# Attention's P times V after every unit of the gated feed-forward, in place of every second unit

## The chip, the cores and the metric

The kernel runs on one core of one Trainium2 chip. Its metric is the device time of one execution in microseconds (us); the kernel before has a median of 2574.44 us over three runs (2574.06 to 2574.53). A core has a matrix engine (TensorE, PE in the profile, with its weight loads shown apart as PEld), a vector engine (VectorE, DVE), an activation engine (ScalarE, ACT), GpSimd (POOL), and SyncE (SP), whose queue issues most of the DMAs here.

## The reference

The input x has 2048 rows of 576 features. It is normalized (layer norm without weights), and the normalized rows feed two branches: softmax attention with 32 heads of 18 features, and a gated feed-forward with 4608 hidden features.

```
xn = layernorm(x)
q, k, v = split(xn @ wqkv)                    # 32 heads of 18
p = softmax(q k^T * 18**-0.5)                 # 2048 x 2048 for each head
s = (p v) @ wo
h = relu(xn @ W_gate) * (xn @ W_up)           # 4608 wide
g = silu(h @ W_down)
out = x + s * g
```

Everything is float32. Most products are taken as three products of split operands (a high part and a rest), which is why each product of the feed-forward shows up three times.

## The kernel before

The program has three stages. The first normalizes the rows, turns them and computes q, k and v, which go to DRAM. The last projects the attention's output with wo, multiplies by the gate and adds x. The long middle stage, from about 200 to 2500 us, runs attention and feed-forward interleaved. All of the change lies there.

**Units.** The feed-forward is cut into 144 units: four groups of 512 rows by 36 blocks of 128 hidden features (`units`). Function `emit_unit` (lines 937 to 992) emits one unit k. It opens with weight loads and splits, then interleaves on TensorE the unit's gate and up products (`up`, tile `pg`, two chains of 27 matmuls that run on the two 64-row halves of the array) with attention work: matmuls of scores for the row maxima of the next head pair (`max_steps`, tile `pm`, reduced by VectorE into `mx`) and matmuls of scores for the exponentials of the present head pair (`exp_steps`, tile `psx`, then an exponential on ScalarE into a tile `p`). A list of due times worked out in `emit_unit` fixes the order. The prediction calls this an up stretch. Then `up_end` applies relu on ScalarE and multiplies on VectorE (line 740), which gives the tile `h`, later split into `hh` (line 747 and GpSimd).

**Rounds of two units.** After the up stretch, what follows depends on whether k is odd or even. For an even k, `down(k - 1)` (line 754) multiplies the hidden features of the two units k - 2 and k - 1 by W_down: 96 matmuls in eight chains (tile `py`), with marks on ScalarE (line 781) where a chain changes banks, and additions of the results into `y` (VectorE at line 797; one of four blocks by ScalarE and GpSimd). For an odd k, `attend` (line 920) empties the list `ready`.

**P times V.** In units 16 to 143 each head pair u takes eight units. Each unit completes four key tiles of 128 keys: for each, the exponentials of two heads by two blocks of 512 queries, in one tile `p` of four parts. `exp_steps` appends such a tile to `ready`. `attend` takes one and issues four matmul calls, one for each part, whose outputs lie in four strips of 32 partitions of one PSUM bank (`po`):

```
for s_ in range(4):
    h = s_ // 2
    mm(
        po[0][s_ * 32 : s_ * 32 + 32, :], va[:, kt, h * VA : h * VA + 32], pt[:, s_, :],
        start=(kt == 0), stop=(kt == NT - 1), skip_group_check=True,
    )
```

As the operands are float32, each call is two matmuls in the profile, so a key tile is eight, in two groups of four that run side by side. Sixteen key tiles make half a head pair (1024 queries); after the last, `finish` copies `po` on ScalarE and puts the rest (transposes, a reciprocal and a product on VectorE, lines 877 to 887) into the list `outs`, which runs just ahead of the next P times V. The stores of the finished block go through the list `later`, which the next `emit_unit` runs (`run_later`).

**What fixes the order.** TensorE's matmuls, VectorE's operations in this stage, GpSimd's operations and a part of ScalarE's are held to program order. The exponentials are not, until the last head pair (`ac`), and SP's DMAs are not after unit 17; a scheduler places these at compile time. The tiles `p` come from a pool of eight buffers (line 688), `po` has one PSUM bank (line 108), and the score and down tiles share five (line 107).

Of the kernel before, what the change touches and what calls it, by code (L numbers as in the profile page):

```python
# [19 lines left out]
def kernel(  # L20
# [46 lines left out]
    def mm(*args, **kw):  # L67
        return tc.keep_in_program_order(nc.tensor.matmul(*args, **kw))  # L68
# [217 lines left out]
    def load_up(k):  # L286
        if k < len(units):
            f = units[k][1]
            if 2 < k < N1:
                rgs[k] = as_rg(pp.tile([P, 4, 512], F32, name="p"))  # L290
            else:
                rgs[k] = wr.tile([P, KC, P], F32, name="rg")
            load2(rgs[k], [[(wg, f * P, P)], [(wu, f * P, P)]])

    def split_up(k):
        if k in rgs:
            gus[k] = ws.tile([P, 2, KC, P], F32R, name="gw")
            split_pool(gus[k][:, 0], gus[k][:, 1], rgs.pop(k))
# [393 lines left out]
    def load_down(k):  # L692
        if k < len(units):
            f = units[k][1]
            if k == 1:
                rds[k] = hp.tile([P, 2, 512], F32, tag="hh", name="rd", bufs=3)
                rds[k] = rds[k].rearrange("p a s -> p (a s)")[:, :D]
            else:
                rds[k] = wl.tile([P, D], F32, name="rd", bufs=1)
            sp.dma_start(rds[k], wd[f * P : (f + 1) * P, :])  # L700

    def split_down(k):
        dws[k] = wl.tile([P, 2, D], F32R, name="dw")
        split_pool(dws[k][:, 0], dws[k][:, 1], rds.pop(k))

    def up(k):

        g, f = units[k]
        gw = gus.pop(k)
        if k < N1 and (k % 2 == 0 or k == N1 - 1):  # L710
            ps = [psO.tile([P, 512], F32, name="po"), shared("pg2")]
        else:
            ps = [bank("pg0"), bank("pg1")]
        last = f == NF - 1 and k + 1 < len(units)
        if f == NF - 2 and k + 2 < len(units):
            for c in range(2):
                load_x(units[k + 2][0], c)
        xg = xcur[g]

        def ops(t, c, i, j, rows):  # L720
            return gw[rows, i, c, :], xg[c][rows, j, :]

        def half(t):
            for n, _ in enumerate(row_half(ps[t], ops, t)):
                c = n // len(PRODUCTS)
                if t and last and n % len(PRODUCTS) == 2 and c + 2 < KC:
                    load_x(units[k + 1][0], c + 2)
                    if c == KC - 3:
                        load_up(k + 2)
                yield  # L730

        return ps, [half(t) for t in range(2)]

    def up_end(k, ps):
        g, f = units[k]
        if f == NF - 1 and k + 1 < len(units):
            del xcur[g]
        h = hp.tile([P, 512], F32, name="h", bufs=1)
        ac.activation(h, ps[0], AF.Relu)
        vec(nc.vector.tensor_tensor(h, ps[1], h, ALU.mult))  # L740
        between.append((split_h, (k, h)))
# [62 lines left out]
    def gate_step(spill_=True):  # L804
        if gates:
            y, t = gates.pop(0)
            e = wl.tile([P, D], F32, name="e", bufs=1)
            tc.keep_in_program_order(nc.scalar.activation(e, y, AF.Tanh, scale=0.5))
            gp.tensor_scalar(e, e, 0.5, 0.5, op0=ALU.mult, op1=ALU.add)
            gp.tensor_tensor(y, y, e, ALU.mult)  # L810
            if spill_:
                gp.dma_start(gd[t * P : (t + 1) * P, :], y)
# [14 lines left out]
    def run_later():  # L827
        while later:
            later.pop(0)()

    outs = []

    def run_tasks(todo):
        while todo:
            fn, args = todo.pop(0)
            fn(*args)
# [34 lines left out]
    def finish(po, u, p):  # L871
        ot = block32("ot")
        ac.activation(ot, po, AF.Copy)

        def rest_():
            tq = block32("tq")
            vec(nc.vector.transpose(tq, ot))
            tv = tq.rearrange("p (c d) -> p c d", d=32)
            rc = two.tile([P, 16], F32, name="rc")
            vec(nc.vector.reciprocal(rc, tv[:, :, DH]))  # L880
            vec(
                nc.vector.tensor_tensor(
                    tv[:, :, :DH], tv[:, :, :DH], rc.unsqueeze(2).to_broadcast([P, 16, DH]), ALU.mult
                )
            )
            on = block32("on")
            vec(nc.vector.transpose(on, tq))
            later.append(lambda: store(on, u, p))

        outs.append((rest_, ()))  # L890

    ready = []
# [27 lines left out]
    def attend():  # L920

        va, u, p, kt, pt = ready.pop(0)
        if kt == 0:
            po[0] = psO.tile([P, 512], F32, name="po")
# [6 lines that stand above are left out]
        if kt == NT - 1:  # L931
            finish(po[0], u, p)
# [4 lines left out]
    def emit_unit(k, ex, ns, mx, nm):  # L937
        if k - 1 in rds:
            split_down(k - 1)
        if k == len(units) - 2:  # L940
            split_up(k + 1)
            out_weights(4)
        if k not in rds and k not in dws:
            load_down(k)
        if k == 0:
            load_down(1)
        split_up(k + 1)
        if k and (units[k][1] < NF - 1 or k + 1 == len(units)):
            load_up(k + 2)
        if k == N1 + 1:  # L950
            sp.kept = False
        run_later()
        if k % 2:
            if k in rds:
                split_down(k)
            for _ in range(2):
                if to_load:
                    out_weights(to_load.pop(0))
        n = KC * len(PRODUCTS) + ns + nm
        ps, gens = up(k)  # L960
        order = []
        for t in range(2):
            due = []
            for cnt, gen, off, late in ((nm, mx, 0.0, LATE), (ns, ex, 0.25, -4)):
                due += [((i + off + t * 0.5) * (n - 1 + late) / cnt, gen[t]) for i in range(cnt)]
            due.sort(key=lambda d: d[0])
            ops = [gens[t]] * n
            free = n
            for when, gen in reversed(due):
                free = min(round(when), free - 1)  # L970
                ops[free] = gen
            order.append(ops)
        for i, (l, r) in enumerate(zip(*order)):
            next(l)
            next(r)
            if i == 8 or (i == 30 and k % 2 == 0):
                gate_step()
        if k == 0:
            split_up(2)
        up_end(k, ps)  # L980
        if k % 2 or k == 0:
            run_tasks(between)
        if k == 0:
            pinned(nc.scalar.activation(first_exp, ident[:, :1], AF.Exp))
        run_tasks(tasks)
        if k % 2:
            run_tasks(outs)
            while ready:
                attend()
        elif k:  # L990
            down(k - 1)


# [2 lines left out]
    def out_weights(c):  # L996
        rd = wl.tile([P, D], F32, name="rd", bufs=1)
        if c < 4:
            sp.dma_start(rd, wo[c * P : (c + 1) * P, :])
            w = kq.rearrange("p c s -> p (c s)")[:, c * 2 * D : (c + 1) * 2 * D]  # L1000
        else:
            for d in range(2):
                sp.dma_start(rd[d * DT : (d + 1) * DT, :], wo[C4:D, :])
            w = wr.tile([P, 2 * D], F32R, tag="rg", name="wo4")
        w = w.rearrange("p (i d) -> p i d", i=2)
        split_pool(w[:, 0], w[:, 1], rd)
        wos.append(w)
# [68 lines left out]
    k = 0  # L1076
    for n in FIRST:
        if 4 <= k < 4 + NQ:
            load_k(1, k - 4)
        emit_unit(k, None, 0, mx, n)  # L1080
        k += 1
    for u in range(NU):
# [8 lines left out]
        for i in range(PER):  # L1091
            if not more and i == 0:
                to_load[:] = range(4)
            emit_unit(k, ex, 64 // PER, mx, 64 // PER if more else 0)
            if not more:
                if i == 3:
# [77 lines left out]
```

## Time and profile before

| What | Value |
| --- | --- |
| Median of three runs | 2574.44 us |
| The profiled execution's own time | 2574.45 us |
| Its span, first to last instruction | 2572.7 us |
| TensorE busy, instructions | 2565.1 us, 25301 |
| P times V on TensorE (`po` from `p` and `va`) | 4096 matmuls, 452.7 us busy |
| Gate and up products (`pg`), the largest group | 1359.2 us busy |
| Down products (`py`) | 478.1 us busy |
| VectorE, ScalarE, GpSimd busy | 1852.5, 1473.8, 1286.7 us |

A row of a group gives the line, the engine, the operation, the tiles written and read with their sizes, the count, the busy time in us with the mean of one in ns, and then the idle time ahead of them. Busy time counts time in which at least one instruction of the group runs, so matmuls that run side by side are counted once, and the mean of one can be longer than its share. A row of the timeline gives the start, the length from the first start to the last end, the engine and the operation, with neighbours of one kind put together (x64). Matmul ends are modelled; the starts are what the arguments here use.

### The profile page before, as it was taken

The numbers are of one execution on the slowest core, as the hardware profiler recorded it, in microseconds if no ns is written. First come the engines' busy times: TensorE is split into PE (matmuls) and PEld (weight loads), VectorE is DVE, ScalarE is ACT, GpSimd is POOL, SyncE is SP. The second block draws the span as 40 slices with busy tenths as digits, with TensorE's granted clock in tenths as the row PEclk, the third lists the DMA queues.
The fourth block names the chain that finished last, engine by engine and source line by source line (L and its number), as shares of the span: only waits on it lengthen the run. The fifth ranks groups of instructions, "written<-read, shape, count | busy, mean of one in ns | idle before, by whom it ended". The sixth has DMA issues, their size and how long they took to land.

```text
span 2572.7 us, 61560 instructions
## 1 busy us (share of the span) xinstructions
PE 2565.1 (100%) x25301; PEld 2039.7 (79%) x25301; DVE 1852.5 (72%) x3019; ACT 1473.8 (57%) x3005; POOL 1286.7 (50%) x1035
## 2 busy tenths in 40 slices
PE   9999999999999999999999999999999999999999
PEld 8889997777777777777777777777777777777788
DVE  5336677777877788877777777887777877778136
ACT  3222146666666666666666666666666666666652
POOL 4246764444465444444465454444445445454554
PEclk9999999999999999999999999999999999999999
DMA  7864432333542223232353232322354332322246
GB/s 249 293 206 126 110 88 51 79 74 76 125 115 68 72 69 75 58 78 65 97 140 85 69 77 63 77 71 63 75 131 107 74 76 66 79 52 59 70 135 199
DMA packets 263833, 253.55 MB, mean 99 GB/s; under 512 B 27648, under 2 KB 208896, under 8 KB 263552
## 3 DMA queue, kind: packets, MB, share of 16 engines
q1 hardware_dynamic: 255808, 222.48, 34.2%
q0 software_dynamic: 7744, 27.14, 3.1%
q8 instruction: 199, 3.26, 0.5%
q14 instruction: 82, 0.67, 0.1%
HBM read 203.01 MB, written 46.01 MB: 97 GB/s over the span
## 4 chain that ended last, share of the span: by engine, by line
PE 98%; DVE 1%; POOL 0%; DMA 0%; issue 0%; ACT 0%; SPq 0%; POOLq 0%; ACTq 0%
PE pg L68 33%; PE po L68 18%; PE py L68 18%; PE pm L68 10%; PE psx L68 10%; PE pq L68 3%; PE pw L68 2%; PE pv L68 2%; PE tps L76 0%; DMA qd<-hh 0%; DMA xt<-in_A_x_dram 0%; POOL gw L85 0%; DVE hh L129 0%; DVE wqk L645 0%; DVE xn L374 0%
## 5 line engine op out<-in xcount | busy, mean ns | idle before, releaser
L273 DVE TENSOR_REDUCE mx<-pm 128x1 f32<-128x512 f32 x2048 | 1372.2, 690 | 355.2 <-PE pm L68 180.8
L68 PE MATMUL pg<-x,gw 64*128 64x512 f32 x7533 | 1359.2, 392 | 0.0
L97 ACT ACTIVATE p<-psx 128x512 f32<-128x512 f32 x2048 | 1097.2, 604 | 202.4 <-PE psx L68 161.7
L68 PEld LDWEIGHTS pg<-x,gw 64*128 64x128 f32 x7533 | 1028.9, 186 | 80.5 <-issue 1.9
L85 POOL TENSOR_TENSOR hh<-h,hh 128x512 fp32r<-128x512 f32 x144 | 185.8, 1290 | 802.5 <-ACT hh L747 798.7
L68 PE MATMUL py<-dw,hh 64*128 64x288 f32 x6912 | 478.1, 293 | 0.0
L68 PEld LDWEIGHTS py<-dw,hh 64*128 64x128 f32 x6912 | 472.8, 184 | 5.4 <-ACT h L97 0.6
L68 PE MATMUL po<-p,va 128*32 128x512 f32 x4096 | 452.7, 594 | 0.0
L68 PEld LDWEIGHTS po<-p,va 128*32 128x32 f32 x4096 | 126.5, 110 | 291.2 <-issue 280.0
L85 POOL TENSOR_TENSOR gw<-rg,gw 128x1152 fp32r<-128x1152 f32 x131 | 349.8, 2670 | 10.5
L797 DVE TENSOR_TENSOR y<-py,y 128x288 f32<-128x288 f32 x422 | 171.8, 453 | 139.3 <-PE py L68 139.2
L68 PE MATMUL psx<-qT,kq 56*128 56x512 f32 x608 | 231.1, 392 | 0.0
L68 PE MATMUL pm<-kq,qT 54*128 54x512 f32 x608 | 225.4, 395 | 0.0
L85 POOL TENSOR_TENSOR dw<-rd,dw 128x576 fp32r<-128x576 f32 x144 | 206.2, 1432 | 11.5
L68 PE MATMUL psx<-kq,kA 56*128 56x512 f32 x512 | 195.8, 393 | 0.0
L68 PE MATMUL psx<-kq 56*128 56x512 f32 x512 | 194.7, 392 | 0.0
L68 PE MATMUL pm<-kA,kq 54*128 54x512 f32 x512 | 191.5, 396 | 0.3 <-DVE mx L273 0.3
L68 PE MATMUL pm<-kq 54*128 54x512 f32 x512 | 191.1, 396 | 0.0
L781 ACT ACTIVATE mark<-ident 128x1 f32<-128x1 f32 x288 | 58.4, 203 | 218.3 <-PE py L68 218.2
L85 POOL TENSOR_TENSOR y<-add,y 128x576 f32<-128x576 f32 x61 | 87.3, 1432 | 187.4 <-ACT add L97 182.0
L85 POOL CAST gw<-rg 128x1152 fp32r<-128x1152 f32 x131 | 154.5, 1179 | 51.0 <-DMA rg<-in_B_W_up_dram 20.6
L747 ACT ACTIVATE hh<-h 128x512 fp32r<-128x512 f32 x144 | 90.7, 630 | 123.9 <-DVE h L740 123.9
(106 smaller groups left out, 2559.3 us busy)
## 6 DMA issues: line engine op xcount, KB each, us to landing
rd<-in_B_W_down_dram SPq DMA_DIRECT2D x144, 288.0 KB
rg<-in_B_W_gate_dram SPq DMA_DIRECT2D x131, 288.0 KB
rg<-in_B_W_up_dram SPq DMA_DIRECT2D x131, 288.0 KB
x<-xTd SPq DMA_DIRECT2D x72, 256.0 KB
qd<-hh POOLq DMA_DIRECT2D x16, 512.0 KB, 4.5
kd<-hh POOLq DMA_DIRECT2D x16, 512.0 KB, 5.8
xTd<-x SPq DMA_DIRECT2D x16, 512.0 KB
kq<-kd SPq DMA_DIRECT2D x210, 36.0 KB
```

Of the source, the lines that this page charges most:

```text
L68: return tc.keep_in_program_order(nc.tensor.matmul(*args, **kw))
L85: return lambda *args, **kw: tc.keep_in_program_order(op(*args, **kw))
L97: i = op(*args, **kw)
L273: vec(nc.vector.tensor_reduce(mx[:, h, b, j, c : c + 1], ps, axis=AX.X, op=ALU.max))
L747: copy = nc.scalar.activation(hhs[k][:, 0], h, AF.Copy)
L781: seen.append(pinned(nc.scalar.activation(mark, ident[:, :1], AF.Copy)))
L797: vec(nc.vector.tensor_tensor(ys[j][:, cs], outs_[m], ys[j][:, cs], ALU.add))
```

## The change

In `emit_unit`, the list `outs` and all of `ready` are worked off at the end of every unit. The down product of an even unit stays, and now follows the unit's P times V. A unit leaves four key tiles in `ready`, so each P times V has four key tiles (32 matmuls in the profile) where every second unit had eight (64).

```
         run_tasks(tasks)
-        if k % 2:
-            run_tasks(outs)
-            while ready:
-                attend()
-        elif k:
+        run_tasks(outs)
+        while ready:
+            attend()
+        if k % 2 == 0 and k:
             down(k - 1)
```

The units before 16 have nothing in `ready` or `outs`; for them nothing is different.

## The prediction

> **What bounds the kernel now.** I read the first page of the profile, then the waits of TensorE, then one round of two units cut into stretches, and last the timeline at the places where TensorE changes from one kind of work to another.
>
> ```profile
> span 2572.7 us, 61560 instructions
> ...
> PE 2565.1 (100%) x25301; PEld 2039.7 (79%) x25301; DVE 1852.5 (72%) x3019; ACT 1473.8 (57%) x3005; POOL 1286.7 (50%) x1035
> ...
> PEclk9999999999999999999999999999999999999999
> ...
> PE 98%; DVE 1%; POOL 0%; DMA 0%; issue 0%; ACT 0%; SPq 0%; POOLq 0%; ACTq 0%
> ...
> L97 ACT ACTIVATE p<-psx 128x512 f32<-128x512 f32 x2048 | 1097.2, 604 | 202.4 <-PE psx L68 161.7
> ...
> L68 PE MATMUL po<-p,va 128*32 128x512 f32 x4096 | 452.7, 594 | 0.0
> ```
>
> TensorE is on 98% of the chain that ended last and its clock is never throttled. A modelled busy share of 100% doesn't say that no time is lost between matmuls, so the view of TensorE's own waits comes next, and one round (all busy times in us; the columns are PE, PEld, DVE, ACT, POOL, clock, DMA share, GB/s).
>
> ```profile
> PE warm L76 <- POOL ident masks.py:199: 1.4, 1, 1.4
> PE tps L76 <- DVE xn L374: 1.3, 2, 1.0
> PE pm L68 <- DVE mx L273: 0.3, 1, 0.3
> ```
>
> ```profile
> 1311.82:1318.24 6.42, 6.42 (x98) 6.42 (x98) 4.48 (x10) 2.04 (x6) 5.48 (x5) 1.00 0.14 39
> 1318.24:1328.65 10.41, 10.41 (x90) 8.39 (x86) 9.23 (x15) 9.86 (x20) 7.42 (x6) 1.00 0.50 125
> 1328.65:1335.65 7.00, 7.00 (x65) 1.98 (x64) 5.10 (x8) 0.91 (x2) 6.51 (x7) 1.00 0.66 168
> 1335.65:1345.80 10.15, 10.15 (x90) 8.33 (x87) 8.71 (x14) 9.19 (x18) 7.01 (x7) 1.00 0.37 96
> ...
> 1379.93:1413.60 33.67, 33.67 (x334) 25.83 (x332) 28.09 (x45) 21.12 (x42) 15.84 (x11) 1.00 0.29 72
> ```
>
> These are the three largest of the five rows of its waits: TensorE waits for other engines under 4 us in the whole run. A round is: the down product (6.42), an up stretch with scores in it (10.41 here, less in most rounds), a burst of P times V over eight key tiles (7.00), another up stretch (10.15). A typical round takes 33.67. So the time is the sum of TensorE's own work, and a change counts by what it does to the spacing of matmuls. The number of matmuls stays the same; what changes is how often TensorE passes between the up or down work, which uses 64-row tiles, and P times V, which uses tiles of 32 columns.
>
> **The change, part by part: what a burst costs beside its matmuls.** These are starts and lengths on TensorE: first the passage from an up stretch to the down product, then into the burst.
>
> ```profile
> 1311.59 0.44 PE L68 MATMUL pm<-kA,kq 54*128 54x512 f32 x2
> 1311.83 6.61 PE L68 MATMUL py<-dw,hh 64*128 64x288 f32 x96
> ...
> 1328.34 0.39 PE L68 MATMUL pm<-kA,kq 54*128 54x512 f32 x1
> ...
> 1329.11 5.33 PE L68 MATMUL po<-p,va 128*32 128x512 f32 x48
> ```
>
> Then the end of the burst and the next up stretch, with the weight loads of the same place below.
>
> ```profile
> 1334.26 1.47 PE L68 MATMUL po<-p,va 128*32 128x512 f32 x12
> 1335.66 0.50 PE L68 MATMUL pm<-kq 54*128 54x512 f32 x1
> ...
> 1336.00 0.39 PE L68 MATMUL psx<-qT,kq 56*128 56x512 f32 x1
> ...
> 1336.46 0.39 PE L68 MATMUL pm<-kq 54*128 54x512 f32 x1
> ```
>
> ```profile
> 1335.66 0.18 PEld L68 LDWEIGHTS pm<-kq 54*128 54x128 f32 x1 [0.84 <-issue]
> ...
> 1335.77 0.19 PEld L68 LDWEIGHTS psx<-qT,kq 56*128 56x128 f32 x1
> ```
>
> The regular step: in the up stretch two row halves run side by side, and from 1336.00 to 1336.46 lie two steps, 0.23 each. From up to down the step is 1311.83 - 1311.59 = 0.24, so this passage costs nothing today. In the burst four matmuls run side by side; 48 take 5.33 and 12 take 1.47, so nine groups of four take 3.86, one 0.429.
>
> Into the burst: it starts at 1328.65 (the third stretch above), 0.31 after the last matmul of the up stretch, 0.08 over the regular step. Out of it: sixteen groups by 0.429 are 6.86, while the stretch to the first up matmul is 7.00: 0.14 goes into filling and emptying. And the first pair after it is longer: 1336.00 - 1335.66 = 0.34 in place of 0.23, 0.11 more. The weight rows show why: no weight load begins for 0.84 until the burst has left the array, and the second load starts only at 1335.77, where elsewhere loads run ahead under the matmuls. One visit to P times V thus costs 0.08 + 0.14 + 0.11 = 0.33 us over its matmuls.
>
> The change replaces one visit of sixteen groups in each round by two of eight (8 x 0.429 + 0.14 = 3.57 each). The rounds run from unit 16 to unit 143, 64 of them, so there are 64 more visits. The new ones end in the down product, not in an up stretch, which this trace doesn't show. The nearest row is the same passage between other kinds of tile, from the projection (full 128-row tiles) to the down product:
>
> ```profile
> 2520.72 0.43 PE L68 MATMUL pw<-wo,o 128*128 128x288 f32 x2
> 2521.08 0.67 PE L68 MATMUL py<-dw,hh 64*128 64x288 f32 x6
> ```
>
> One down step is (6.61 - 0.29) / 47 = 0.134, with 0.29 the part of the 0.43 that the last matmul alone takes (0.43 - 0.134 gives the same). The second projection matmul starts at about 2520.86, the down product 0.22 later, 0.09 over a step; three pairs then take 0.67 where 2 x 0.134 + 0.29 = 0.56 were due, 0.11 more. That is 0.20, against 0.14 + 0.11 = 0.25 out of P times V. So a new visit costs between 0.08 + 0.20 = 0.28 and 0.33. I take 0.33, since the visit leaves the same burst. 64 x 0.33 = 21.1 us.
>
> The Trainium skill has two rules here that pull apart. Its page "TensorEngine Tiling (Array Packing)", under Key Properties, says that a change of tiling mode (not merely of tile) drains TensorE; it speaks against this change, and the 0.84 without a weight load agrees. "TensorE: Matmul & The Clock Gate", Part 2, says that the drain of one matmul, some 128 cycles, overlaps the fill of the next; by a bare drain of 128 cycles at 2.4 GHz, 53 ns twice in a visit, the estimate from that page would be 64 x 0.107 = 6.8 us.
>
> **The rest, costed at nothing, with its cover.** The new burst uses only key tiles of its own unit, so TensorE waits for ScalarE's exponentials where it did not before; behind that wait stands the whole down product.
>
> ```profile
> 1309.77 1.77 ACT L97 ACTIVATE p<-psx 128x512 f32<-128x512 f32 x3
> ...
> 1326.92 1.27 ACT L97 ACTIVATE p<-psx 128x512 f32<-128x512 f32 x2
> ...
> 2447.09 2.69 ACT L97 ACTIVATE p<-psx 128x512 f32<-128x512 f32 x5
> ```
>
> In an even unit the last exponential ends at 1309.77 + 1.77 = 1311.54, before the up stretch ends (1311.83); in an odd one at 1328.19, before 1328.65. In the last eight units it ends at 2449.78, in a round whose down product began at 2449.25 as the next row shows; there only the fourth key tile is late, by 0.53, and it is needed 6 groups, 2.57 us, into the burst. Cover: 2.0 us at the least, so no wait.
>
> ```profile
> 2449.25 0.57 PE L68 MATMUL py<-dw,hh 64*128 64x288 f32 x6
> ```
>
> The down product moves behind the new burst with all it issues: 96 matmuls, four marks on ScalarE, the additions of VectorE, ScalarE and GpSimd, and no DMA. The finishing of a head pair (two transposes, reciprocal, product on VectorE) moves from the odd burst to the even one before it, and its output stores move one unit earlier in SP's queue.
>
> ```profile
> 1309.49 4.02 DVE L273 TENSOR_REDUCE mx<-pm 128x1 f32<-128x512 f32 x6
> 1313.44 0.68 DVE L740 TENSOR_TENSOR h<-pg,h 128x512 f32<-128x512 f32 x1
> 1314.48 1.62 DVE L797 TENSOR_TENSOR y<-py,y 128x288 f32<-128x288 f32 x4 [0.36 <-PE py L68]
> ```
>
> ```profile
> 1330.11 0.68 DVE L740 TENSOR_TENSOR h<-pg,h 128x512 f32<-128x512 f32 x1
> 1330.70 0.70 DVE L877 STREAM_TRANSPOSE tq<-ot 128x512 f32<-128x512 f32 x1
> 1331.44 0.26 DVE L880 RECIPROCAL rc<-tq 128x16 f32<-128x16 f32 x1
> 1331.73 1.38 DVE L882 TENSOR_TENSOR tq<-tq,rc 128x288 f32<-128x288 f32 x1
> 1333.14 0.71 DVE L887 STREAM_TRANSPOSE on<-tq 128x512 f32<-128x512 f32 x1
> ```
>
> In the even unit VectorE is free at 1314.12, with the finishing (3.05) at 1317.2; the first additions of the down product, at 1314.48 today, come 3.57 + 0.09 later, at 1318.1. Cover 0.9 us. In the odd unit VectorE ends the up stretch's product at 1330.79, and the next up stretch, now at 1328.65 + 3.57 = 1332.2, still finds it idle. Without that cover each late microsecond would cost 32 us (two head-pair halves in each of 16 head pairs). GpSimd, with 15.84 busy in 33.67, only sees its work for the down product shift. SP waits for the finished block already:
>
> ```profile
> SPq L97 <- DVE on L887: 79.4, 27, 4.4
> ```
>
> What stands behind it there, weight loads and key strips, is waited for by nobody on TensorE, by the view of waits above; bounds -1 to +2 us, taken as 0. The profiled execution took 2574.45 us, its span being 2572.7 and the rest outside it, against a median of the runs of 2574.44. Sum: 2574.45 + 21.1 = 2595.5 us, slower by 0.82%.
>
> **The rivals.** *Faster: the pause pays.* Between up and down the other engines get 3.6 us in which TensorE needs nothing of them; if waits inside the up stretches go and the switch costs nothing, time falls. What could go: a round of 33.67 less burst 7.00 and down 6.42 leaves 20.25 for two up stretches, less the 0.08 and 0.11 of the visit 20.06; 86 steps of 0.23 are 19.8, so at most 0.28 x 64 = 18 us, 2556.5. It decides when a visit costs less than it removes. Against it: an up stretch behind a burst, where the others have had 7 us of rest, takes 10.15 - 0.11 = 10.04, and one behind the down product, by the typical round, 20.25 - 10.15 - 0.08 = 10.02. The rest buys nothing. Chance 0.03.
>
> *No change: the new passage is hidden*, the down product's weight loads running under the burst's last group, and the entry by the shorter waits at the odd burst. 2574.5, within 5 us. The 0.84 of no weight load speaks against it, and it occurs at nearly every visit:
>
> ```profile
> PEld pm L68 <- issue: 49.5, 59, 0.8
> ```
>
> Chance 0.04. By the second rule of the skill above the time would be 2574.45 + 6.8 = 2581.3, which lies between this case and mine.
>
> *Much slower: ScalarE's order.* Its exponentials are not held to program order; if the last six of an even unit fell behind the activation that waits for the end of the up stretch (0.60, as any of this size), they would end 7 x 0.60 = 4.2 us after it, 1.6 past the cover of 2.57, and 64 x 1.6 = 104 us would come to the 21: 2700. It decides from four on (5 x 0.60 = 3.0). Against it: the rows above, where the exponentials at even and odd units alike end ahead of that activation or beside it. Chance 0.03. *VectorE late at the finishing*, one microsecond past its cover of 0.9: 21 + 32 us: 2628; chance 0.03.
>
> **How the numbers follow.** Mine has 0.87: 2595.5. Its own ends: the exit to the down product half hidden (0.10 in place of 0.25) gives 64 x 0.18 = 11.5 and 2586; 32 finishings late by a quarter of a microsecond give 8 more, 2604. The other cases hold 0.13, so the range stays at 2586 to 2604. A measurement of this kernel can tell about 0.2%, 5.1 us, from no change. Faster 0.03, same 0.04, slower 0.93.
>
> **What would show it.** The changed profile should have a burst of 32 matmuls at the end of every unit, first burst to next work 3.57; the passage from burst to down product some 0.25 over its regular step, with no weight load for about 0.8; rounds of 34.0 in place of 33.67; up stretches unchanged at 10.0; no new entry in TensorE's waits. Waits of po for ScalarE, a down product longer than 6.6 to its next stretch, or rounds not over 33.7 would make me wrong.

## The result, and the profile after

The changed kernel takes 2605.78 us (median of three runs, 2604.92 to 2607.07), against 2574.44 before: 1.0119 times as long, with a 95% interval of 1.0106 to 1.0132. That is 31.3 us slower. The forecast was slower by 21.1, to 2595.5, with a range that ended at 2604. The direction was right, the size a third too small.

The first page of the changed kernel:

```profile
span 2603.2 us, 61552 instructions
...
PE 2589.7 (99%) x25301; PEld 1997.0 (77%) x25301; DVE 1826.7 (70%) x3019; ACT 1468.7 (56%) x3005; POOL 1284.1 (49%) x1035
...
PE 95%; DMA 2%; POOL 1%; DVE 1%; issue 0%; ACT 0%; SPq 0%; POOLq 0%; ACTq 0%
PE pg L68 31%; PE py L68 18%; PE po L68 18%; PE pm L68 10%; PE psx L68 9%; PE pq L68 4%; PE pw L68 2%; PE pv L68 2%; DMA x<-xTd 2%; POOL gw L85 0%; PE tps L76 0%; POOL y L85 0%; DMA xt<-in_A_x_dram 0%; DMA rd<-in_B_W_down_dram 0%; SPq L97 0%
```

The number of matmuls is the same. TensorE's share of the last chain has fallen from 98 to 95%, and loads of x tiles have 2%, which they did not have before. A regular round, cut at the down product, the up stretch of the odd unit, its burst, the up stretch of the even unit and its burst (columns as in the prediction):

```profile
1401.11:1407.61 6.50, 6.50 (x101) 6.50 (x98) 2.92 (x7) 1.33 (x5) 1.30 (x1) 1.00 0.12 30
1407.61:1417.75 10.14, 10.14 (x90) 8.59 (x87) 9.44 (x15) 9.31 (x19) 8.91 (x7) 1.00 0.12 32
1417.75:1421.32 3.57, 3.57 (x34) 0.94 (x32) 2.14 (x4) 1.14 (x2) 1.07 (x2) 1.00 1.06 242
1421.32:1431.57 10.25, 10.25 (x91) 8.55 (x87) 9.23 (x14) 8.73 (x17) 4.35 (x3) 1.00 0.38 90
1431.57:1435.14 3.57, 3.57 (x35) 0.94 (x33) 2.13 (x4) 0.50 (x1) 0.00 (x0) 1.00 0.12 40
```

Two bursts of 3.57, as forecast. Seven such rounds in a row, first before, then after:

```profile
806.80:1042.49 235.69, 235.69 (x2326) 183.24 (x2324) 186.22 (x301) 150.16 (x298) 112.87 (x89) 1.00 0.30 74
```

```profile
819.62:1057.61 237.99, 237.99 (x2330) 177.30 (x2326) 184.78 (x303) 149.43 (x298) 112.66 (x89) 1.00 0.30 73
```

A round takes 235.69 / 7 = 33.67 before and 237.99 / 7 = 34.00 after: 0.33 more, and 64 rounds make 21.1. The passage from the burst to the down product, which the trace of before did not hold, looks as the one to the up stretch did (timeline of the weight loads):

```profile
1435.14 0.97 PEld L68 LDWEIGHTS py<-dw,hh 64*128 64x128 f32 x14 [0.84 <-issue]
```

So the other 10 us lie outside the regular rounds. TensorE's own waits in the changed kernel name their causes; neither of these rows was there before:

```profile
PE pm L68 <- ACT p L97: 3.8, 3, 2.5
PE pg L68 <- DMA x<-xTd: 3.3, 6, 0.9
```

All of them lie at the three places where the feed-forward goes over to the next 512 rows, that is around the units 36, 72 and 108. The idle time in these rows, 7.1 us, understates the loss there. The two rounds at the first change, from the down product in unit 34 to the one in unit 38, before and then after:

```profile
671.30:738.98 67.68, 67.68 (x666) 51.92 (x663) 53.18 (x87) 43.73 (x88) 39.22 (x34) 1.00 0.58 134
```

```profile
676.81:751.37 74.56, 71.29 (x669) 50.27 (x666) 52.20 (x86) 43.72 (x88) 40.72 (x35) 0.98 0.55 131
```

They are 6.88 longer; the pairs of rounds at the second and the third change, measured in the same way, are 3.64 and 3.99 longer (67.62 to 71.26 and 67.64 to 71.63). That is 14.5, or 12.5 more than six visits at 0.33. The visits, in turn, hold some 2 us less than 64 x 0.33: the rounds just behind a change, and the first one, lose only 0.11 to 0.14, and the three rounds of the last head pair, which have no scores for row maxima, lose nothing (before, then after):

```profile
2388.97:2479.39 90.42, 90.42 (x903) 69.44 (x901) 20.26 (x36) 60.36 (x133) 57.71 (x43) 1.00 0.34 86
```

```profile
2423.21:2513.57 90.36, 90.36 (x904) 65.89 (x900) 17.42 (x33) 60.57 (x131) 57.58 (x43) 1.00 0.35 87
```

So the loss is nearer to 19 us for the visits and 12.5 at the changes of rows than to 21 and 10. (These sum to 1 us above the difference of the two spans, as the first down product starts 1.0 earlier in the profile after.) What happens at the changes of rows is of two kinds.

**The tiles of x.** The nine chunks of x for the next rows are loaded in 18 DMAs of 256 KB, four of them in advance and the others during the last up stretch, as it frees the buffers. SP's queue before, where the next up stretch begins at 1301.72, and after, where it begins at 1315.79:

```profile
1289.65 9.93 SPq L304 DMA_DIRECT2D x<-xTd  x14
```

```profile
1307.11 10.18 SPq L304 DMA_DIRECT2D x<-xTd  x14
```

Before, the issue of the last of them ends at 1299.58, 2.1 us ahead of the up stretch for the new rows; after, at 1317.29, 1.5 us behind its start. Of the 3.6 us between, 3.43 are what the odd burst became shorter by. TensorE then catches up with the loads:

```profile
1315.79 0.50 PE L68 MATMUL pm<-kq 54*128 54x512 f32 x1
...
1324.70 0.49 PE L68 MATMUL pg<-x,gw 64*128 64x512 f32 x1 [0.72 <-DMA x<-xTd]
...
1326.70 0.74 PE L68 MATMUL pg<-x,gw 64*128 64x512 f32 x4 [0.56 <-DMA x<-xTd]
...
1328.06 0.64 PE L68 MATMUL po<-p,va 128*32 128x512 f32 x4
```

This up stretch takes 1328.06 - 1315.79 = 12.27, where a regular one behind a burst takes 10.25.

**The gate.** Two units later, in unit 38, the gate of the finished rows (line 808: a hyperbolic tangent on ScalarE into the tile e, then products on GpSimd) holds up the exponentials. GpSimd, ScalarE and TensorE in the changed kernel:

```profile
731.39 0.66 POOL L85 CAST dw<-rd 128x576 fp32r<-128x576 f32 x1 [4.12 <-DMA rd<-in_B_W_down_dram]
...
742.53 1.40 POOL L85 TENSOR_TENSOR y<-y,e 128x576 f32<-128x576 f32 x1
```

```profile
743.96 0.68 ACT L808 ACTIVATE e<-y 128x576 f32<-128x576 f32 x1 [2.92 <-POOL y L85]
```

```profile
745.18 0.50 PE L68 MATMUL pm<-kq,qT 54*128 54x512 f32 x1 [2.51 <-ACT p L97]
```

GpSimd waits 4.12 for a down weight, works through its queue, and is done with the tile e at 743.93; ScalarE's next tangent needs that single buffer and waits 2.92 for it; the exponentials queued behind the tangent are late, and a score matmul finds no free bank for 2.51. Before, GpSimd waited as long for the same load (4.20), but its product ended at 736.82 and the tangent ran at 736.88, with no wait in its row: with 7 us of burst in between, the queue was just in time. The up stretch of unit 38 began at 728.83, 4.78 behind GpSimd's cast of the weight (724.05); after, it begins at 732.83, 1.44 behind it. The 3.34 between are again those of the shorter burst. GpSimd and ScalarE before:

```profile
724.05 0.66 POOL L85 CAST dw<-rd 128x576 fp32r<-128x576 f32 x1 [4.20 <-DMA rd<-in_B_W_down_dram]
...
735.38 1.44 POOL L85 TENSOR_TENSOR y<-y,e 128x576 f32<-128x576 f32 x1
```

```profile
736.88 0.71 ACT L808 ACTIVATE e<-y 128x576 f32<-128x576 f32 x1
```

The stall has a second price, in TensorE's clock. This is the up stretch of unit 38 after, with the burst behind it (the third number from the end is the granted clock):

```profile
732.83:746.10 13.27, 10.76 (x91) 8.24 (x87) 9.03 (x14) 9.40 (x19) 12.27 (x12) 1.00 0.43 112
746.10:751.37 5.27, 5.27 (x35) 1.29 (x34) 2.10 (x4) 0.49 (x2) 1.54 (x2) 0.68 0.40 142
```

The burst takes 5.27 in place of 3.57, for 3.4 us of it at half the clock: 1.7 of the 12.5 us.

### The profile page after: what moved, and what is told of

It reads as the page before. It is cut to its first block, busy times and chain, and to the rows that moved or that the text cites. A ratio compares the mean times of both kernels' runs of the same rounds, so it can differ in the third digit from the quotient of the medians.

```text
span 2603.2 us, 61552 instructions
## 1 busy us (share of the span) xinstructions
PE 2589.7 (99%) x25301; PEld 1997.0 (77%) x25301; DVE 1826.7 (70%) x3019; ACT 1468.7 (56%) x3005; POOL 1284.1 (49%) x1035
## 4 chain that ended last, share of the span: by engine, by line
PE 95%; DMA 2%; POOL 1%; DVE 1%; issue 0%; ACT 0%; SPq 0%; POOLq 0%; ACTq 0%
PE pg L68 31%; PE py L68 18%; PE po L68 18%; PE pm L68 10%; PE psx L68 9%; PE pq L68 4%; PE pw L68 2%; PE pv L68 2%; DMA x<-xTd 2%; POOL gw L85 0%; PE tps L76 0%; POOL y L85 0%; DMA xt<-in_A_x_dram 0%; DMA rd<-in_B_W_down_dram 0%; SPq L97 0%
## 5 line engine op out<-in xcount | busy, mean ns | idle before, releaser
L68 PEld LDWEIGHTS pg<-x,gw 64*128 64x128 f32 x7533 | 1013.4, 186 | 112.0 <-DMA x<-xTd 6.0
L68 PEld LDWEIGHTS py<-dw,hh 64*128 64x128 f32 x6912 | 465.4, 184 | 54.2 <-issue 29.5
L68 PE MATMUL po<-p,va 128*32 128x512 f32 x4096 | 467.7, 597 | 0.0
L68 PEld LDWEIGHTS po<-p,va 128*32 128x32 f32 x4096 | 120.3, 110 | 277.6 <-issue 267.1
L68 PE MATMUL pm<-kA,qT 54*128 54x512 f32 x416 | 157.1, 397 | 0.0
```

## The experiments

Theory A, from these lines: a visit to P times V costs 0.33 in every round, and the halved odd burst uncovers the loads and the gate at the three changes of rows, 10 us. Theory B: a visit costs 31.3 / 64 = 0.49. Theory C: the finishing and its stores, one unit earlier, are to blame. Times are medians; each of the two groups of four kernels shared runs of the kernel before, at 2574.63 and 2574.51.

| Kernel | us | Ratio to before, 95% interval |
| --- | --- | --- |
| after | 2605.78 | 1.0119 (1.0106 to 1.0132) |
| e1, long odd burst kept at the changes | 2592.11 | 1.0069 (1.0052 to 1.0085) |
| e2, split at the changes alone | 2588.35 | 1.0053 (1.0039 to 1.0068) |
| e3, three visits in a round | 2623.00 | 1.0188 (1.0173 to 1.0204) |
| e4, one key tile and seven | 2600.89 | 1.0103 (1.0088 to 1.0118) |
| e5, x loaded further ahead | 2593.65 | 1.0073 (1.0058 to 1.0088) |
| e6, x ahead and two tiles e | 2593.91 | 1.0074 (1.0058 to 1.0089) |
| e7, two tiles e | 2599.71 | 1.0096 (1.0079 to 1.0112) |
| e8, finishing at odd units | 2627.43 | 1.0203 (1.0188 to 1.0218) |

**e1: the long odd burst kept at the changes of rows.** Against the kernel after:

```
-        run_tasks(outs)
-        while ready:
-            attend()
+        if not (k % 36 in (0, 34) and k < 140):
+            run_tasks(outs)
+            while ready:
+                attend()
```

> The kernel after, but without a burst in the units 34, 36, 70, 72, 106 and 108, so that the odd units behind them (35, 37 and so on, at the change to the next 512 rows) have bursts of eight key tiles again. Theory A: a visit to P times V costs 0.33 us in every round, and the other 10 us of the loss come from the halved odd bursts at the three changes of rows, which had covered the loads of x for the next rows and GpSimd's gate work. Then the 10 us come back, with 6 visits less: 2605.8 - 10.2 - 2.0 = 2593.6. Theory B: a visit simply costs 31.3 / 64 = 0.49: 2605.8 - 6 x 0.49 = 2602.9. Theory C: the finishing and the stores, one unit earlier, upset VectorE or SP's queue: 2604, since they stay early.

Measured 2592.11, as theory A had it. B and C fall: six bursts of 128 hold 13.7 us. In TensorE's waits both new rows are gone. What is left, 2592.11 - 2574.63 = 17.5, is 0.30 for each of 58 additional visits on the average (the three of the last head pair that cost nothing are among them).

**e2: the split at the changes of rows alone.** Against the kernel before, the condition of the burst is widened:

```
-        if k % 2:
+        if k % 2 or (k % 36 in (0, 34) and k < 140):
             run_tasks(outs)
             while ready:
                 attend()
-        elif k:
+        if k % 2 == 0 and k:
             down(k - 1)
```

> The other part alone: the kernel before, with the additional burst only in the units 34, 36, 70, 72, 106 and 108. Theory A: 2574.4 + 6 x 0.33 + 10.2 = 2586.6. Theory B: 2574.4 + 6 x 0.49 = 2577.4. Theory C: 2575 to 2577, as only one head-pair half in ten finishes earlier.

Measured 2588.35: 13.7 us from six bursts. Its waits are those of the kernel after:

```profile
PE pm L68 <- ACT p L97: 3.9, 2, 2.5
PE pg L68 <- DMA x<-xTd: 3.9, 6, 1.0
```

Together e1 and e2 make 17.5 + 13.7 = 31.2, all of the change's 31.3, though the interval of each is some 4 us wide on either side.

**e3: three visits in a round.** Against the kernel after:

```
-        while ready:
+        while len(ready) > (0 if k % 2 else 2):
             attend()
         if k % 2 == 0 and k:
             down(k - 1)
+            while ready:
+                attend()
```

> The kernel after, but the even unit's burst in two parts of two key tiles, one ahead of the down product and one behind it: three visits in a round in place of two, the odd bursts unchanged. Theory A: 64 visits more at 0.33, the waits at the changes of rows as they were: 2605.8 + 21.1 = 2627. Theory B: 64 x 0.49 more: 2637. Theory C says nothing of its own beyond 0.33 a visit: 2627.

Measured 2623.00 (2620.95 to 2625.62), 17 us over the kernel after. In its trace seven regular rounds take 240.30, so 34.33 each: 0.33 more for one more visit, as for the first one, though this one passes from the down product into the burst and on to an up stretch. The total is 4 short of 64 x 0.33, but the runs spread over 4.7 us. The profiled one, at 2625.62, is 20.7 above the profiled one of the kernel after (2604.92), and its rounds at the changes of rows are 14.7 longer than before, where those of the kernel after are 14.5 longer: the additional visits make the difference.

```profile
822.58:1062.88 240.30, 240.30 (x2328) 179.06 (x2324) 183.37 (x301) 150.17 (x298) 112.46 (x89) 1.00 0.30 72
```

**e4: one key tile at the even unit, seven at the odd.** Against the kernel before:

```
-        if k % 2:
-            run_tasks(outs)
+        run_tasks(outs)
+        if k % 2:
             while ready:
                 attend()
-        elif k:
-            down(k - 1)
+        else:
+            if ready:
+                attend()
+            if k:
+                down(k - 1)
```

> As many visits as in the kernel after, but the even unit's burst has one key tile and the odd one seven; the finishing moves to the even unit as in the kernel after. Theory A: 64 visits at 0.33, and the odd burst gives up 0.86 us of its cover only, so that little or nothing is waited for at the changes of rows: 2574.4 + 21.1 + 0 to 2.5 = 2595.5 to 2598. Theory B: 2606. Theory C: 2605, as the finishing is early here too.

Measured 2600.89, a miss by 3 to 5 us. The waits for x and for the exponentials are indeed gone, but three others are there, one at each change of rows. Waits and timeline of TensorE, then VectorE and GpSimd:

```profile
PE py L68 <- DVE y L797: 4.1, 3, 1.7
```

```profile
1330.61 4.54 PE L68 MATMUL py<-dw,hh 64*128 64x288 f32 x36 [1.68 <-DVE y L797]
```

```profile
1326.76 2.70 DVE L882 TENSOR_TENSOR tq<-tq,rc 128x288 f32<-128x288 f32 x1
1329.50 0.71 DVE L887 STREAM_TRANSPOSE on<-tq 128x512 f32<-128x512 f32 x1
1330.13 1.51 DVE L797 TENSOR_TENSOR y<-py,y 128x288 f32<-128x288 f32 x4
```

```profile
1326.46 2.68 POOL L85 TENSOR_TENSOR gw<-rg,gw 128x1152 fp32r<-128x1152 f32 x1
```

With an even burst of 1 us the finishing on VectorE runs into the down product. Its product takes 2.70 at this place, since GpSimd works until 1329.14, and the down product waits for banks that VectorE frees late. A short burst on either side uncovers something else.

**e5: x loaded further ahead.** Against the kernel after, two more buffers for x, paid with one of the eight tiles p:

```
-    xA = pool(early, "xA", KC + 2)
+    xA = pool(early, "xA", KC + 4)
...
-    pp = pool(mid, "pp", 8, "right")
+    pp = pool(mid, "pp", 7, "right")
...
-            for c in range(2):
+            for c in range(4):
                 load_x(units[k + 2][0], c)
...
-                if t and last and n % len(PRODUCTS) == 2 and c + 2 < KC:
-                    load_x(units[k + 1][0], c + 2)
-                    if c == KC - 3:
+                if t and last and n % len(PRODUCTS) == 2 and c + 4 < KC:
+                    load_x(units[k + 1][0], c + 4)
+                    if c == KC - 5:
```

> The kernel after, with two more buffers for x tiles (eleven to thirteen) and so four in place of two chunks of the next 512 rows loaded ahead of the change; the room comes from one buffer of the tiles p (eight to seven). Theory A1, two separate causes at a change of rows: the waits for x in units 36, 72 and 108 go (about 5 us), those of the gate work two units later stay: 2600.7. Theory A2, one cause: the loads of x also hold up what stands behind them in SP's queue, and with them done sooner the gate work is in time as well: 2595.6. If the loads of x are not the matter: 2605.8.

Measured 2593.65, which is A2: one cause. In unit 38 GpSimd no longer waits for the load of the down weight, and the tangent is in time. GpSimd and ScalarE in e5:

```profile
727.02 0.67 POOL L85 CAST dw<-rd 128x576 fp32r<-128x576 f32 x1 [0.54 <-PE pm L68]
...
738.18 1.44 POOL L85 TENSOR_TENSOR y<-y,e 128x576 f32<-128x576 f32 x1
```

```profile
740.12 0.71 ACT L808 ACTIVATE e<-y 128x576 f32<-128x576 f32 x1
```

SP issues this weight in the kernel after and then in e5 at

```profile
726.81 0.37 SPq L97 DMA_DIRECT2D rd<-in_B_W_down_dram  x1
```

```profile
723.49 0.37 SPq L97 DMA_DIRECT2D rd<-in_B_W_down_dram  x1
```

that is 6.0 us and 8.6 us ahead of the up stretch of unit 38, which begins at 732.83 and at 732.06. Between the loads of x and this one stand, in SP's queue, gate and up weights: GpSimd begins to split them at 710.74 in the kernel after and at 707.63 in e5, and the next loads of that kind, ahead of the one shown, follow when it is done with them, at 714.88 and at 711.53.

What is left over the kernel before, 19.1 us (14.9 to 22.7 by the interval), is 0.30 (0.23 to 0.35) for each of the 64 additional visits on the average. No run has seven tiles p alone; that e6, with six, takes the same time as e5 speaks against these tiles having a part in it.

**e7: two buffers for the gate's tile.** Against the kernel after (and seven tiles p):

```
-            e = wl.tile([P, D], F32, name="e", bufs=1)
+            e = wl.tile([P, D], F32, name="e2", bufs=2)
```

> The kernel after, with two buffers in place of one for the gate's tile e, apart from the sums that shared it (and seven tiles p in place of eight): ScalarE's hyperbolic tangent needs not wait for GpSimd to have used the one before, and the exponentials behind it are in time. Theory A1: the waits in units 38, 74 and 110 go (about 5 us) and those for x stay: 2600.5. If ScalarE's wait for that buffer is not what holds the exponentials: 2605.8.

Measured 2599.71, 6.1 us better than the kernel after, as it should be if ScalarE's wait for the buffer held the exponentials. In the trace (of the slowest of its four runs, 2602.56) the third change shows it: a tangent begins at 1974.10, while the product on the tile before ends only at 1976.63. At the first change one buffer would have done in this trace, since the up stretch that waits for x took 14.14 there and gave GpSimd time. Of the two new rows in TensorE's waits only that of x is left:

```profile
PE pg L68 <- DMA x<-xTd: 3.6, 6, 1.0
```

**e6: both remedies,** with six tiles p.

> Both remedies together (six tiles p): by theory A both waits at the changes of rows go and only the 64 additional visits are left: 2574.4 + 21.1 = 2595.5, to 2597. By theory B (0.49 for each visit, whatever the buffers): 2605.8.

Measured 2593.91, the same as e5. With x in time, the second buffer has nothing left to do.

**e8: the finishing back at the odd units.** Against the kernel after:

```
-        run_tasks(outs)
+        if k % 2:
+            run_tasks(outs)
         while ready:
             attend()
```

> The kernel after, with the finishing of a head-pair half back at the odd units, so that only P times V itself is as in the change. Theory A: nothing of the 31 us hangs on it: 2605.8. Theory C: a part of the 10 us comes back, to 2596 at the most.

Measured 2627.43, 21.7 slower than the kernel after, which no theory said. The odd burst of 3.57 is too short for the finishing. VectorE, TensorE and the waits of the weight loads in e8 (a burst ends at 666.25 here):

```profile
665.76 1.39 DVE L882 TENSOR_TENSOR tq<-tq,rc 128x288 f32<-128x288 f32 x1
667.18 0.71 DVE L887 STREAM_TRANSPOSE on<-tq 128x512 f32<-128x512 f32 x1
667.82 2.67 DVE L273 TENSOR_REDUCE mx<-pm 128x1 f32<-128x512 f32 x4
```

```profile
668.52 0.50 PE L68 MATMUL pm<-kq,qT 54*128 54x512 f32 x1 [0.62 <-DVE mx L273]
```

```profile
PEld pm L68 <- DVE mx L273: 32.7, 34, 2.4
```

VectorE comes to the row maxima of the next up stretch 1.57 us after it has begun, and TensorE waits for a bank. This happens some 30 times. Of the 1.57, 0.93 come from GpSimd: the product of line 882 takes 1.39 beside it here, and 0.46 at the even unit in the kernel after (last section). So theory C has the sign wrong: that the change also moves the finishing to the even unit, where the down product needs VectorE only later, saves it 22 us.

## Why the prediction was right or wrong

- *What bounds the kernel, and a visit's price:* right. 0.33 a round was forecast and 0.33 is what the regular rounds show, also for a third visit (e3). By the times of e1 and e5 it is 0.30 on the average, since not every round pays it; so 64 x 0.33 = 21.1 was some 2 us too large, which hid as much of the loss elsewhere. The 0.84 us without a weight load stand at the new passage as at the old one. The Trainium skill's page "TensorEngine Tiling (Array Packing)", under Key Properties, by which a change of tiling mode drains TensorE, agrees with these rows. The 6.8 us estimated from the Trainium skill's page "TensorE: Matmul & The Clock Gate", Part 2, did not come: a visit costs 0.33 in a regular round, not 0.107.
- *The passage to the down product,* bounded by 0.28 and 0.33 a visit: right, at the upper end.
- *ScalarE's exponentials,* with a cover of 2 us: right in the regular rounds. At unit 38 in the profile they were late, yet not by their order, as the rival had it, but by the gate's tangent in front of them.
- *The finishing on VectorE,* costed at nothing: right, with some luck, as the product of line 882 took 0.46 at the even unit in place of the 1.38 that was counted. What lost cover costs, e8 shows at the odd burst: 21.7 us for 32 finishings, 0.68 each, with VectorE 1.57 late at the place shown.
- *The step that failed* is that of the rest at nothing, where the text says of weight loads behind the stores in SP's queue that they are "waited for by nobody on TensorE, by the view of waits above". That view is of the kernel before, where the odd burst of 7 us was the cover. The odd burst was costed for VectorE alone, in a regular round; the three changes of rows, which the trace of before also holds, were not looked at. There the halved burst uncovers the loads of x and, behind them in SP's queue, the down weight that GpSimd, the gate and ScalarE wait for. The term taken as 0 measured 12.5 us in the trace of the kernel after, and about 12 by e1 and e2 (13.7 less six visits) and by e5 (12.1 less than the kernel after). 1.7 of it is a clock granted at half behind a stall, a term that the forecast did not have. "Up stretches unchanged at 10.0; no new entry in TensorE's waits" failed with it.
- *The rival of a pause that pays* did not come about: an up stretch behind a burst is no shorter (10.25) than one behind the down product (10.14).

No kernel tried here beats the one before: in each of them the additional visits remain.

## What to carry to other kernels

A stretch in which one engine works alone is cover for everything else, and shortening or moving it has to be costed at the tightest place of the program, not in a regular round: look at each boundary of the outer loops for transfers that only just arrive. A view of waits says what is late now, not how much room the rest has; read the room as the time from the last issue or landing to the first use. And where small tiles of another shape are mixed into a stream of matmuls, count the visits and price one from the trace.

## What the runs showed of the hardware

The same VectorE product of the finishing (line 882, two operands from SBUF) took between 0.46 and 2.85 us in these runs. The view of its tile gives the shortest, median and longest in ns, before and then after:

```profile
L882 DVE TENSOR_TENSOR tq<-tq,rc x32: 458/1388/1625, 455.1 to 2522.6; 128x288 f32<-128x288 f32 x32
```

```profile
L882 DVE TENSOR_TENSOR tq<-tq,rc x32: 458/459/2845, 438.3 to 2553.2; 128x288 f32<-128x288 f32 x32
```

The difference is whether GpSimd works at the time. VectorE and GpSimd before, where they meet, and VectorE after, where GpSimd does nothing at that time:

```profile
589.86 1.40 DVE L882 TENSOR_TENSOR tq<-tq,rc 128x288 f32<-128x288 f32 x1
```

```profile
589.65 1.28 POOL L85 TENSOR_TENSOR hh<-h,hh 128x512 fp32r<-128x512 f32 x1 [2.52 <-ACT hh L747]
```

```profile
574.33 0.46 DVE L882 TENSOR_TENSOR tq<-tq,rc 128x288 f32<-128x288 f32 x1
```

GpSimd's product begins first and ends at 590.93, VectorE's ends at 591.26, 0.33 later, which is less than the 0.46 it takes alone; in e4 it ends 0.32 after the GpSimd product that ran beside it. The Trainium skill's page "SBUF — State Buffer", in "SBUF: two separate sides", says that VectorE with two SBUF inputs and a GpSimd instruction that reads SBUF take a shared pair of ports by an exclusive lock: the one that starts first has it for its whole instruction, and the other blocks. These rows agree. The forecast had taken 1.38 for this product, a wait in GpSimd's company, as its duration.

TensorE's granted clock fell to half for 3.4 us at a stall at a change of rows, once in the profiled executions of the kernel after, e2, e4, e7 and e8, and for twice as long in e3. In the kernel after, it fell 1.3 us behind the end of the stall of 2.51. In the profiles of the kernel before, e1, e5 and e6, which have no such stall, the middle stage shows the full clock throughout. Not every stall was followed by a slower clock, and what decides was not isolated.
